# Batch 0's softmax and first weight block, the last quarter's products in halves, and one output transfer on GpSimd's queue

## The chip, the cores and the metric

The kernel runs on one core of one Trainium2 chip. The metric is the device time of one execution in microseconds (us). Three executions of the kernel before took 265.26, 265.31 and 265.31 us, median 265.31 us. The trace and the profile page are of one further execution, which took 265.6 us; the span in its records, from the first instruction to the last, is 263.6 us. All times inside the kernel are us from the start of that span.

## The reference

Linear attention is followed by a two-layer perceptron. There are 8 batches, 8 heads, 576 rows and head dimension 64, so that the model dimension is 512; the hidden dimension is 2048.

```python
def _attn_ref(q, k, v):
    q_s = np.exp(q - max_over_d); q_s = q_s / (sum_over_d + 1e-09)
    k_s = np.exp(k - max_over_s); k_s = k_s / (sum_over_s + 1e-09)
    kv = np.einsum('bhsd,bhse->bhde', k_s, v)
    return np.einsum('bhsd,bhde->bhse', q_s, kv)

def _moe_ref(x, g_ln, w_ch1, w_ch2):      # x: (8, 576, 512)
    mu, var = mean and variance of x over its last axis
    xn = (x - mu) / np.sqrt(var + 1e-06) * g_ln
    ch = np.maximum(xn @ w_ch1, 0.0) @ w_ch2
    return x + ch
```

All inputs and the output are float32.

## The kernel before

**Tiling.** Each batch has 512 main rows, kept as 128 partitions by T = 4 quarters; the remaining 64 rows of all eight batches are collected in a ninth batch, C9, which is worked on last. The products run in bf16. The program walks over the batches 0 to 7 and C9; `run` (L775) merges a list of main steps (the matmuls of the MLP, each with a weight that stands for its duration) with a list of side jobs (attention of the next batch, loads, weight preparation), each with the place at which it is put between the main steps. The order on every engine is that of the program text as it is recorded (L1026).

**Queues.** SyncE (SP) issues q's first half and the four quarters of k of batch 0 (L901, L912), later loads, DMA transposes and half of the last stores. ScalarE (ACT) issues g and the other half of the last stores. GpSimd (POOL) issues, in this order: v of batch 0 in three pieces (L931), q's second half (L901), w1 in five pieces that are cast to bf16 on the way (two of 256 columns, three of 512, L92), w2 and the loads of batch 1 and 2, and later the output of batches 0 to 7 (L474, L561). Each of these queues keeps its order.

**The front (first_batch, L888 to L989).** Memsets, then `warm` (L789): matmuls on a scratch tile that keep TensorE running. Then for quarters 0 and 1 `exp_qt` (ACT), the exponentials of k by pairs of heads `exp_k0` (L262), `norm_q` (DVE), transposes of eq on TensorE with a copy to `eqT` by ACT or DVE (`eq_pT`, L877 with `pe_T`, L857), the column sums of k's exponentials (`z0_mm`, L268), g's columns (`g_columns`, L883), the products of keys and values (`kv0_mm`, L284; after every second pair two DVE rows write `kv_sb`, L297), the attention products of quarters 0 and 1 in column halves (`po_half`, L391; ACT copies them to `x`, L402), the centring `xn_out` (L372), and the first transposes to `xnT` (L983).

**The first MLP stage (mlp_steps, L745; mm1_part, L443).** Batch 0's first products go by parts (m0, mn, t0, tn): blocks m0 to m0 + mn of the hidden dimension, quarters t0 to t0 + tn, each over the four 128-row slices ko of w1. The first four parts take blocks 0 to 3 and quarters 0 and 1, two blocks and one quarter at a time. Quarters 2 and 3 pass as side jobs between them (L1045 to L1049): transposes of eq and xn, the sums `z_q` and products `po_mm` (`q0_rest`, L991), and `x_fast` (L380).

**The tail (last_products, L574).** C9's second MLP product runs as seven products of half size (Strassen's form) into PSUM banks a to e. The last product, n = 4, is added to bank a for the third quarter and to a bank d of its own for the fourth, 8 matmuls of 256 columns each; a DVE row (`stt`, L584) adds it to `yl`, and `store` (L589) writes 64 partitions through SP and 64 through ACT.

At the very end every engine drains and meets at a barrier (L1119); SP first checks the semaphores of all transfers one after the other.

Of the kernel before, what the change touches and what calls it, by code (L numbers as in the profile page):

```python
# [20 lines left out]
def kernel(  # L21
# [21 lines left out]
    P = 128  # L43
# [302 lines left out]
    def po_mm(c, t, i):  # L346


        if i == 0:
            pool, tag = (mm_ps, "m") if c == 0 and t >= 2 else (att_ps, "a")  # L350
            pobox["p"] = pobox[c, t] = pool.tile([P, DM], FP32, tag=tag, name="po")
        if c < B:
            nc.tensor.matmul(  # L353
                pobox["p"][:, i * P : i * P + P], eqTs[c][:, t, i, :], kv_sb[:, c, i, :],
                start=True, stop=True,
            )
        else:
            for half in range(2):
                ps = slice(64 * half, 64 * half + 64)
                nc.tensor.matmul(  # L360
                    pobox["p"][ps, i * P : i * P + P], eqTs[c][:, t, i, ps],
                    kv_sb[:, 2 * t + half, i, :], start=True, stop=True,
                )
# [26 lines left out]

    def po_half(t, half):  # L391

        pool, tag = (mm_ps, "m") if half else (att_ps, "a")
        po = pool.tile([P, DM], FP32, tag=tag, name="po")
        for i in range(2):
            j = 2 * half + i
            nc.tensor.matmul(
                po[:, i * P : i * P + P], eqTs[0][:, t, j, :], kv_sb[:, 0, j, :],
                start=True, stop=True,
            )  # L400
        x, st, _, _ = xs[0]
        nc.scalar.activation(  # L402
            x[:, t, DH2 * half : DH2 * half + DH2], po[:, 0:DH2], AF.Copy,
            accum_out=st[:, t, half : half + 1],
        )
# [121 lines left out]
        )[i]  # L527
        nc.vector.tensor_tensor(out=dst, in0=x, in1=y, op=op)  # L528

    def prod(n, bank, t, k, first=False, own=False):  # L530

        at = slice(t * P, t * P + P)
        if n in (1, 2, 4):
            odd, half = ((0, 0), (1, 0), None, (1, 1))[n - 1]
            lhsT = hbox["h"][:, 2 * k + odd, 2 * half + t, :]
        else:
            lhsT = hbox["s"][:, {5: 0, 6: 1, 7: 2, 3: 3}[n], k, at]
        if n in (1, 2):
            rhs = w2_sb[:, 2 * k + n - 1, 0:DH2]
        elif n == 3:  # L540
            rhs = w2_sb[:, 2 * k + 1, DH2:DM]
        else:
            rhs = w2_q[:, {5: 0, 6: 1, 7: 2, 4: 3}[n], k]
        nc.tensor.matmul(hbox[bank][:, t], lhsT, rhs, start=first and (own or t == 0) and k == 0,  # L544
                         stop=k == KH - 1, skip_group_check=True)

    def bank(name):
# [26 lines left out]
    def last_products(product):  # L574
# [4 lines left out]
        def part(t, col):  # L579
            return yl[:, t, DH2 * col : DH2 * col + DH2]  # L580

        def stt(t, col, src, add=None):
            cols = slice(DH2 * col, DH2 * col + DH2)
            nc.vector.scalar_tensor_tensor(  # L584
                part(t, col), in0=src, scalar=rstds[c][:, t : t + 1],
                in1=xs[c][0][:, t, cols] if add is None else add, op0=ALU.mult, op1=ALU.add,
            )

        def store(t0, tn, col):  # L589
            cols = slice(DH2 * col, DH2 * col + DH2)  # L590
            for half, eng in enumerate((nc.sync, nc.scalar)):
                ps = slice(64 * half, 64 * half + 64)
                to = out[2 * t0 + half : 2 * (t0 + tn) - 1 + half : 2, SM:S, cols]
                eng.dma_start(to.transpose([1, 0, 2]), yl[ps, t0 : t0 + tn, cols])
# [8 lines left out]
        def seed_e():  # L603
# [10 lines left out]
        product(7, "a", at={1: [seed_e, lambda: both("b", 2, 1)], 15: [  # L614
            lambda: both("a", 2, 1, True), lambda: stt(3, 0, hbox["a"][:, 1]),
            lambda: store(2, 2, 1)]})
        product(3, "e", at={15: [lambda: both("e", 0, 1), lambda: store(0, 2, 1), own_bank]})
        product(4, "a", ts=(0,), at={7: [lambda: stt(2, 0, hbox["a"][:, 0]), lambda: store(2, 1, 0)]})
        product(4, "d", ts=(1,), own=True, at={
            15: [lambda: stt(3, 0, hbox["d"][:, 1], part(3, 0)), lambda: store(3, 1, 0)]})  # L620

    def mm2_fast(c):

        steps = []

        def product(n, name, first=False, at=None, ts=range(2), own=False, cut=None):
            at = at or {}
            order = [(t, k) for t in ts for k in range(KH)]
            if cut:
                order = [(t, k) for ks in (range(cut), range(cut, KH)) for t in ts for k in ks]  # L630
            for i, (t, k) in enumerate(order):

                def go(t=t, k=k, i=i):
                    if i == 0 and first:
                        bank(name)
                    prod(n, name, t, k, first or own, own)
                    for fn in at.get(i + KH * ts[0], []):
                        fn()

                steps.append((0.5, go))  # L640

        def seed_c():
            bank("c")
# [101 lines left out]
    def mlp_steps(c):  # L745
# [3 lines left out]
        first, parts = [], ()  # L749
        if c == 0:  # L750
            full = range(0)
            parts = ((0, 2, 0, 1), (0, 2, 1, 1), (2, 2, 0, 1), (2, 2, 1, 1), (4, 4, 0, 2), (0, 4, 2, 1),
                     (0, 4, 3, 1), (4, 4, 2, 2), (8, 4, 0, 2), (8, 4, 2, 2), (12, 4, 0, 2), (12, 4, 2, 2))
        else:
            full, parts = range(8, KO2), ((0, 8, 0, 2), (0, 8, 2, 2))
        for m0, mn, t0, tn in parts:
            first += [
                (0.25 * tn, lambda m=m, t0=t0, tn=tn, ko=ko: mm1_part(c, m, t0, tn, ko))
                for m in range(m0, m0 + mn) for ko in range(KO1)
            ]  # L760
# [127 lines left out]
    def first_batch():  # L888
# [43 lines left out]
                v0[:, j : j + jn].rearrange("p j t d -> p j (t d)"), src0(v, j, jn)  # L932
            )
        load_q0(1, nc.gpsimd)
        load_w1(0, 256)
        load_w1(256, 256)
        for nb in range(1, 4):
            load_w1(512 * nb)
        load_w2(0)
# [1 line left out]

        new_eq(0)
        start_x(0)
        warm(31)
        for t in range(2):
            exp_qt(0, t)
        exp_k0(0)
        exp_k0(1)
        norm_q(0, 0)
        norm_q(0, 1)  # L950
        eq_pT(0, 0, nc.scalar)
        g_columns()
        exp_k0(2)
        warm(5)
        z0_mm(0)
        z0_mm(1)
        exp_k0(3)
        eq_pT(0, 1, nc.vector)
        z0_mm(2)
        warm(3)  # L960
        z0_mm(3)
        recip_z()
        for j in range(NP):
            kv0_mm(j)
        warm(2)
        po_half(0, 0)
        warm(3)
        po_half(0, 1)
        po_half(1, 0)
        po_half(1, 1)  # L970
# [55 lines left out]
    with tc.manual_schedule(  # L1026
# [10 lines left out]
        def po_x(c, t):  # L1037
            for i in range(NP):
# [4 lines left out]
            mlp_steps(0),  # L1043
            [
                (2, lambda: (eq_pT(0, 2, nc.scalar), xn_pT(0, 1, nc.vector), eq_pT(0, 3, nc.scalar))),  # L1045
                (2, lambda: (q0_rest(2), x_fast(0, 2))),
                (6, lambda: q0_rest(3)),
                (8, lambda: (xn_pT(0, 2, nc.vector), x_fast(0, 3))),
                (16, lambda: xn_pT(0, 3, nc.vector)),  # L1049
                (22, lambda: square_sum(0, 0)),  # L1050
                (26, lambda: square_sum(0, 1)),
# [13 lines left out]
            + [(103 + 0.4 * j, lambda j=j: cast_v(1, j)) for j in range(2)]  # L1065
            + [(104.5, lambda: prep_kvrem(1))]
            + [(106, lambda: (kv_all(1), start_x(1)))]
            + [(111, lambda: po_x(1, 0)), (113, lambda: po_x(1, 1))]
            + [(116, lambda: po_x(1, 2)), (118, lambda: xn_pT(1, 0, nc.scalar)), (119, lambda: square_sum(1, 0))]
            + [(119.5, lambda: po_x(1, 3)), (123, lambda: xn_pT(1, 1, nc.scalar)), (124, lambda: square_sum(1, 1))]  # L1070
            + [(128, lambda: xn_pT(1, 2, nc.scalar))]
# [52 lines left out]
```

## Time and profile before

| what | value |
|---|---|
| median of three executions | 265.31 us |
| profiled execution | 265.6 us |
| its span | 263.6 us |
| TensorE (PE) busy | 257.4 us, 98% |
| PE weight loads (PEld) | 218.1 us, 83% |
| VectorE (DVE) | 217.4 us, 82% |
| ScalarE (ACT) | 178.8 us, 68% |
| GpSimd (POOL) | 76.0 us, 29% |
| DMA, chain that ended last | 4% |
| granted PE clock | 1.00, 0.89 behind 259.5 us |

How to read it: a profile line of the chain or of the timeline begins with the start and the duration in us, then the engine, the source line (L451 is line 451 of the kernel before), the operation with output and input, and the number of instructions merged into it; in brackets stands the idle time before it and what ended it. In the table of stages a line holds the stretch, its length, the busy time of PE, PEld, DVE, ACT and POOL with the number of instructions, the granted clock, the busy share of the DMA engines and GB/s. A DMA issue line gives the number of issues, KB of each, and the median us from issue to landing. PE rows overlap: a 128-column matmul is shown with some 0.22 us, though the next one starts 0.055 us later.

### The profile page before, as it was taken

How to read it: one execution, taken by the hardware profiler on the slowest of the kernel's cores; microseconds unless marked ns; L12 is line 12 of the kernel's file. 1: busy time of each engine (PE TensorE's matmuls, PEld its weight loads, DVE VectorE, ACT ScalarE, POOL GpSimd, SP SyncE). 2: the span in 40 equal slices, each digit the busy share in tenths (PEclk: the TensorE clock that was granted, in tenths of full speed). 3: DMA queues.
4: the chain of work that ended last, by engine and by line, in shares of the span. 5: the costliest groups of instructions: out<-in, count | busy, mean ns of one | idle time of the engine just before them, and what ended most of it. 6: DMA issues, size and time to landing. Idle time of an engine off the chain costs nothing.

```text
span 263.6 us, 6818 instructions
## 1 busy us (share of the span) xinstructions
PE 257.4 (98%) x2708; PEld 218.1 (83%) x2711; DVE 217.4 (82%) x475; ACT 178.8 (68%) x350; POOL 76.0 (29%) x126
## 2 busy tenths in 40 slices
PE   8989999999999999999999999999999999999993
PEld 5778855775988998899889988998899888888882
DVE  4667797968989997989798979997999889877873
ACT  4467852896966888688868886788678377438400
POOL 8652316203049007600760076008200300030000
PEclk9999999999999999999999999999999999999999
DMA  6999999997986995799879957997804620521014
GB/s 219 256 204 208 338 208 315 271 155 233 207 151 197 325 136 97 197 308 155 93 215 298 139 99 237 297 135 146 256 6 79 161 82 12 71 90 72 0 42 119
DMA packets 69847, 45.00 MB, mean 171 GB/s; under 512 B 41460, under 2 KB 66040, under 8 KB 69816
## 3 DMA queue, kind: packets, MB, share of 16 engines
q1 hardware_dynamic: 48896, 21.76, 39.3%
q0 software_dynamic: 20320, 22.29, 38.9%
q10 hardware_dynamic: 600, 0.53, 0.6%
q8 instruction: 21, 0.34, 0.6%
q14 instruction: 10, 0.08, 0.1%
HBM read 36.70 MB, written 9.44 MB: 175 GB/s over the span
## 4 chain that ended last, share of the span: by engine, by line
PE 92%; DMA 4%; POOL 2%; issue 0%; ACT 0%; DVE 0%; POOLq 0%
PE ba L544 21%; PE bx L688 19%; PE bb L688 9%; PE ph L451 8%; PE bb L544 5%; PE be L544 5%; PE bc L544 5%; PE pc L497 5%; PE bc L688 5%; DMA w_raw<-in_moe_w_ch_dram 4%; PE ph L436 3%; PE po L353 3%; PE pkv L316 2%; PE ptr L860 1%; POOL v L931 1%; PE po L360 1%
## 5 line engine op out<-in xcount | busy, mean ns | idle before, releaser
L544 PEld LDWEIGHTS <-hs 128*128 128x128 bf16 x512 | 49.5, 98 | 5.7
L688 PEld LDWEIGHTS <-w_q 128*128 128x128 bf16 x448 | 43.1, 98 | 5.2 <-issue 0.2
L544 PEld LDWEIGHTS <-hT 128*128 128x128 bf16 x384 | 37.2, 98 | 4.4
L240 POOL TENSOR_TENSOR tq<-xnT 128x256 bf16<-128x256 bf16 x20 | 12.9, 661 | 78.6 <-DMA xnT<-xn 47.2
L688 PEld LDWEIGHTS <-w1g 128*128 128x128 bf16 x336 | 32.2, 98 | 3.9
L544 PE MATMUL ba<-w_q,hs 128*128 128x256 bf16 x256 | 31.7, 273 | 0.0
L688 PE MATMUL bx<-tq,w_q 128*128 128x256 bf16 x224 | 29.0, 273 | 0.0
L561 POOL DMA_DIRECT2D out_dram<-ot x28 | 15.3, 557 | 46.4 <-DVE ot L555 46.4
L367 ACT ACTIVATE scrap<-x,mv 128x512 bf16<-128x512 bf16 x36 | 25.9, 719 | 1.7 <-DVE x L383 1.3
L383 DVE SCALAR_TENSOR_TENSOR x<-po,rq 128x512 bf16<-128x512 f32 x34 | 23.3, 685 | 1.2 <-PE po L353 1.1
L712 ACT COPY bc<-bx 128x512 f32<-128x512 f32 x28 | 15.2, 594 | 13.0 <-PE bx L688 13.0
L719 DVE TENSOR_TENSOR bb<-bx,s 128x512 f32<-128x512 f32 x28 | 18.2, 694 | 6.3 <-ACT s L716 6.3
L730 ACT ACTIVATE hT<-bc 128x512 bf16<-128x512 f32 x28 | 15.3, 595 | 11.9 <-PE bc L688 11.9
L202 DVE TENSOR_REDUCE zq<-eq 128x16 f32<-128x1024 bf16 (+1 forms) x20 | 20.6, 1049 | 2.3 <-ACT eq L193 2.3
L528 DVE TENSOR_TENSOR hs<-hT 128x1024 bf16<-128x1024 bf16 x32 | 20.9, 674 | 0.9 <-ACT hT L730 0.5
L730 ACT ACTIVATE hT<-bb 128x512 bf16<-128x512 f32 x28 | 15.2, 595 | 8.8 <-PE bb L688 8.8
L353 PE MATMUL po<-kv_sb,eqT 128*128 128x128 bf16 x120 | 20.5, 219 | 0.0
L722 DVE TENSOR_TENSOR hT<-bx,s 128x512 bf16<-128x512 f32 x28 | 18.0, 684 | 3.0 <-PE bx L688 3.0
L569 ACT COPY s<-ba 128x512 f32<-128x512 f32 x15 | 8.7, 579 | 12.5 <-PE ba L544 7.8
L544 PE MATMUL ba<-w_sb,hT 128*128 128x256 bf16 x128 | 16.7, 273 | 0.0
L544 PE MATMUL bb<-w_q,hs 128*128 128x256 bf16 x128 | 16.6, 273 | 0.0
L497 PE MATMUL pc<-w_sb,hT 128*128 128x512 bf16 x61 | 15.6, 379 | 0.2
(135 smaller groups left out, 536.9 us busy)
## 6 DMA issues: line engine op xcount, KB each, us to landing
out_dram<-ot POOLq DMA_DIRECT2D x32, 256.0 KB, 5.9
qt<-in_q_dram SPq DMA_DIRECT2D x5, 1024.0 KB, 7.1
kt<-in_k_dram SPq DMA_DIRECT2D x5, 1024.0 KB, 15.0
vt<-in_v_dram POOLq DMA_DIRECT2D x7, 512.0 KB, 14.3
w_sb<-in_moe_w_ch_dram POOLq DMA_DIRECT2D x4, 512.0 KB, 16.1
qt<-in_q_dram POOLq DMA_DIRECT2D x2, 1024.0 KB, 14.8
kt<-in_k_dram POOLq DMA_DIRECT2D x2, 1024.0 KB, 14.3
w_raw<-in_moe_w_ch_dram POOLq DMA_DIRECT2D x3, 512.0 KB, 13.1
```

The costliest lines, as they stand in the source:

```text
L202: nc.vector.reduce_sum(eqs[c][1][:, ts], eqs[c][0][:, ts], axis=AX.X)
L353: nc.tensor.matmul(pobox["p"][:, i * P : i * P + P], eqTs[c][:, t, i, :], kv_sb[:, c, i, :], start=True, stop=True,)
L367: nc.scalar.activation(scrap, x[:, t], AF.Square, bias=mv[:, t, 0:1], scale=-float(DM), accum_out=mv[:, t, 1:2],)
L383: nc.vector.scalar_tensor_tensor(x[:, t].rearrange("p (h d) -> p h d", h=H), in0=pobox[c, t].rearrange("p (h d) -> p h d", h=H), scalar=1. ...
L451: nc.tensor.matmul(ph[:, m % 2, at : at + tn], (w1g if c else w1_sb)[:, ko, m * P : (m + 1) * P], xnTs[c][:, t0 : t0 + tn, ko, :], start=( ...
L497: nc.tensor.matmul(hbox["pc", t], hbox["h"][:, ko, t, :], w2_sb[:, ko, :], start=(ko == 0), stop=(ko == KO2 - 1),)
L528: nc.vector.tensor_tensor(out=dst, in0=x, in1=y, op=op)
L544: nc.tensor.matmul(hbox[bank][:, t], lhsT, rhs, start=first and (own or t == 0) and k == 0, stop=k == KH - 1, skip_group_check=True)
L688: nc.tensor.matmul(dst[:, q], lhsT, rhs, start=first and q == 0 and ko == 0, stop=ko == 1, skip_group_check=True)
L719: nc.vector.tensor_tensor(out=at[g, "b"], in0=at[g, "x"], in1=at[g, "s"], op=ALU.add)
L722: nc.vector.tensor_tensor(out=h_out(g, 1, 1), in0=at[g, "x"], in1=at[g, "s"], op=ALU.add)
L730: nc.scalar.activation(h_out(g, odd, half), at[g, name], AF.Relu)
```

## The change

- In the front the warm matmuls are divided anew (16, then g's columns, then 16, and fewer later); all four exponentials of k stand together ahead of the first eqT copy on ACT; both eqT copies are made by ACT; the sums z of all four pairs come ahead of the second transposes of eq; and the products of keys and values go pair by pair with warm matmuls between them. `po_half` of quarter 1 takes its PSUM tiles from the pool mm_ps, `po_mm` of batch 0 from att_ps.
- w1's first 512 columns come in two pieces by rows (ko 0 and 1, then ko 2 and 3), not by columns.
- The first MLP products of quarters 0 and 1 run by halves of ko: all four blocks with ko 0 and 1, then all four with ko 2 and 3. The side jobs between them move from places 2, 2, 6, 8 to 2, 4, 8, 8.
- Batch 1's first attention product moves from place 111 to 111.7.
- The last eight matmuls of 256 columns become sixteen of 128, by column halves, and the DVE row behind them becomes two rows of 128 columns; the first stands behind the first eight.
- The store of quarters 0 and 1, second column half, of C9 is issued by GpSimd for both partition halves, not by SP and ACT.

```diff
     def po_half(t, half):
-        pool, tag = (mm_ps, "m") if half else (att_ps, "a")
+        pool, tag = (mm_ps, "m") if half or t else (att_ps, "a")
...
-    def prod(n, bank, t, k, first=False, own=False):
+    def prod(n, bank, t, k, first=False, own=False, ch=None):
...
+        dst = hbox[bank][:, t]
+        if ch is not None:
+            cols = slice(P * ch, P * ch + P)
+            dst, rhs = dst[:, cols], rhs[:, cols]
...
+        def last_half(half):
+            cols = slice(P * half, P * half + P)
+            nc.vector.scalar_tensor_tensor(
+                yl[:, T - 1, cols], in0=hbox["d"][:, 1, cols], scalar=rstds[c][:, T - 1 : T],
+                in1=yl[:, T - 1, cols], op0=ALU.mult, op1=ALU.add,
+            )
...
-        def store(t0, tn, col):
+        def store(t0, tn, col, engs=(nc.sync, nc.scalar)):
...
-        product(3, "e", at={15: [lambda: both("e", 0, 1), lambda: store(0, 2, 1), own_bank]})
+        product(3, "e", at={15: [lambda: both("e", 0, 1), lambda: store(0, 2, 1, (nc.gpsimd, nc.gpsimd)), own_bank]})
...
-        product(4, "d", ts=(1,), own=True, at={
-            15: [lambda: stt(3, 0, hbox["d"][:, 1], part(3, 0)), lambda: store(3, 1, 0)]})
+        product(4, "d", ts=(1,), own=True, half=0, at={15: [lambda: last_half(0)]})
+        product(4, "d", ts=(1,), own=True, half=1, at={15: [lambda: last_half(1), lambda: store(3, 1, 0)]})
...
-            parts = ((0, 2, 0, 1), (0, 2, 1, 1), (2, 2, 0, 1), (2, 2, 1, 1), (4, 4, 0, 2), (0, 4, 2, 1),
+            parts = ((4, 4, 0, 2), (0, 4, 2, 1),
...
+            first += [
+                (0.25, lambda m=m, t=t, ko=2 * kh + ko: mm1_part(c, m, t, 1, ko))
+                for t in range(2) for kh in range(2) for m in range(4) for ko in range(2)
+            ]
...
-        load_w1(0, 256)
-        load_w1(256, 256)
+        for kh in range(2):
+            ks = slice(2 * kh, 2 * kh + 2)
+            nc.gpsimd.dma_start(w1_sb[:, ks, 0:512], w1_src[:, ks, 0:512])
...
-        warm(31)
+        warm(16)
+        g_columns()
+        warm(16)
         for t in range(2):
             exp_qt(0, t)
-        exp_k0(0)
-        exp_k0(1)
+        for j in range(NP):
+            exp_k0(j)
         norm_q(0, 0)
         norm_q(0, 1)
+        z0_mm(0)
         eq_pT(0, 0, nc.scalar)
...
+        z0_mm(1)
+        warm(3)
+        z0_mm(2)
+        z0_mm(3)
+        eq_pT(0, 1, nc.scalar)
+        recip_z()
+        kv0_mm(0)
+        kv0_mm(1)
+        warm(1)
+        kv0_mm(2)
+        warm(2)
+        kv0_mm(3)
+        po_half(0, 0)
         warm(5)
...
-                (2, lambda: (q0_rest(2), x_fast(0, 2))),
-                (6, lambda: q0_rest(3)),
-                (8, lambda: (xn_pT(0, 2, nc.vector), x_fast(0, 3))),
+                (4, lambda: (q0_rest(2), x_fast(0, 2))),
+                (8, lambda: (q0_rest(3), xn_pT(0, 2, nc.vector), x_fast(0, 3))),
...
-            + [(111, lambda: po_x(1, 0)), (113, lambda: po_x(1, 1))]
+            + [(111.7, lambda: po_x(1, 0)), (113, lambda: po_x(1, 1))]
```

## The prediction

> **What bounds the kernel now.** I read the table of stages first, then the chain that ended last, then the waits of the first 22 us, the DMA answers of short windows, and the last rows of every engine. All times are us from the start of the span of before.
>
> ```profile
> 0.00:15.24 15.24, 13.71 (x219) 10.19 (x220) 8.19 (x25) 7.95 (x18) 11.10 (x23) 1.00 0.99 232
> 15.24:21.04 5.80, 5.53 (x81) 4.85 (x81) 4.33 (x13) 3.07 (x6) 2.55 (x3) 1.00 1.24 207
> 21.04:31.80 10.76, 10.76 (x116) 9.86 (x117) 7.26 (x14) 8.39 (x20) 2.71 (x4) 1.00 1.16 276
> 77.00:247.00 170.00, 169.98 (x1773) 150.99 (x1771) 149.26 (x317) 124.84 (x245) 48.06 (x79) 1.00 0.69 151
> 259.50:264.00 4.50, 0.00 (x0) 0.00 (x0) 0.43 (x1) 0.00 (x0) 0.00 (x0) 0.89 0.42 117
> ```
>
> The second column is the length of a stage, the third TensorE's busy time. From 21 to 259.5 TensorE is busy all the time, so a shorter front or a shorter tail comes out in full. No other place of this kernel can pay.
>
> ```profile
> 5.78 9.41 DMA w_raw<-in_moe_w_ch_dram
> 15.24 0.73 PE ph L451 x8
> 16.24 0.59 ACT eqT L862
> 16.88 0.25 PE zs L872 x4
> 21.04 0.40 PE ptr L860 x4
> 258.54 0.89 PE bd L544 x8
> 259.45 0.48 DVE yl L584
> ```
>
> These are pieces of the chain: TensorE starts the MLP at 15.24 when w1's first piece lands (5.78 + 9.4 = 15.2), stands from 16.64 to 16.88 for ScalarE's copy of eqT, and from 20.86 to 21.04 for `xn`; behind the last product come one VectorE row of 0.48 and 3.7 of stores and checks.
>
> ```profile
> 8.37 1.42 ACT L266 ACTIVATE ek<-kt 128x576 bf16<-128x576 f32 x2
> 10.85 1.30 PE L291 MATMUL pkv<-v,ek 64*64 64x64 bf16 x72
> 20.63 0.35 DVE L375 TENSOR_SCALAR xn<-x,mv 128x512 bf16<-128x512 bf16 x1
> q0 software_dynamic: 378, 0.20, 141.5%
> q0 software_dynamic: 208, 0.21, 125.5%
> L1119 POOLq DRAIN  x3: 51/93/6313, 236.4 to 263.3; - x3
> ```
>
> The first three rows are used below. The q0 lines are GpSimd's DMA queue from 12 to 13 (packets of 512 B) and from 17 to 18 (1024 B). The last is GpSimd's drain at its end: 6.3 us.
>
> **The change, part by part.**
>
> *Softmax of the keys, products by pairs.* k's last quarter is issued at 2.8 and lands 6.3 later, at 9.1; ScalarE's last exponential so ends at 9.8 in both kernels (8.37 + 1.42). Before, the 18 z matmuls behind it start only at 10.54 and the 72 products run from 10.85 to 12.09 (17 ns each). After: z at 9.84 (18 of 18 ns, to 10.17), four transposes (0.23, to 10.4), 36 products to 11.05, one warm matmul (0.11), 18 products to 11.47, two warm matmuls (0.22), the last 18 from 11.69 to 12.00. v's pieces land at 9.9, 10.5 and 11.4 (issued 2.96 to 4.4, 6.7 to 7.0 each), so none is late. VectorE's second pair of kv rows (0.59) starts at 12.16 and not 12.25. The four ScalarE copies of `po` follow it: the second starts at 13.11 and not 13.20. So this part is worth only **0.09** at the first half of xnT: it is ready at 15.0, before at 15.1. The warm matmuls are 52 for 53; ScalarE's two eqT copies now stand behind the exponentials (9.8 to 11.0), and nobody asks for them before 12.0.
>
> *w1's first block in row halves.* Per piece 256 descriptors of 1024 B written, before 512 of 512 B. From the q0 lines 512 small packets take 512/378 = 1.35, 256 large ones 256/208 = 1.23: 0.12 a piece. Packet time alone (1.415 x 16 / 378 = 60 ns against 1.255 x 16 / 208 = 97 ns) would give 512 x 60 / 16 = 1.9 against 1.55, 0.35 a piece; nothing gained is the other end. I take 0.12, since the queue's rate is what a landing follows. First piece at 15.1, second (15.9 before) at 15.7. TensorE starts at 15.14: **0.10** gained. The eight matmuls of the first half need only the first half of xnT, so the wait of 0.13 inside the first eight (15.81 - 15.24 - 8 x 0.055) goes.
>
> *Order of the next 5 us.* After the first eight matmuls (0.44, to 15.6) come the three groups of transposes; the middle one waits for `xn` of quarter 1 (15.8, VectorE) to 15.85, the third ends at 16.3. The eight matmuls of the second half (to 16.73) now stand where TensorE waited for eqT (ready 16.5). zs and po: 0.33, to 17.06; sixteen matmuls of 55 ns to 17.94; zs and po to 18.27; xnT's third transposes wait for `xn` (17.28 + 0.70 + 0.39 = 18.37) and end at 18.62, where before stood 19.10. The next sixteen (1.76) need w1's second block, landed at 18.4 before and 18.2 now. VectorE's row for xnT, `x` and `xn` (0.69 + 0.70 + 0.37) follows the transposes, so `xn` of quarter 3 ends at 20.55, before at 20.98. **Gain of the front 0.45**; between 0.1 (only the first step) and 0.65 (that step and the three waits whole, 0.13 + 0.24 + 0.18).
>
> What is late next: the w1, w2 and q loads come only 0.2 earlier. Batch 1's krem lands at 41.35 and its exponential ends at 41.9; TensorE would want it at 42.05 (42.49 before). That is the smallest cover, and it holds.
>
> *po_x at 111.7.* One more mm2 stands ahead of batch 1's first po, which waited 0.14 for kv (43.84 to 43.98). I take **0.1**, between 0 and 0.14. The pools of po and po_half change; the built order shows no wait on a late reader for them.
>
> *The tail.* Column halves: sixteen matmuls of 55 ns for eight of 109, the same 0.87. VectorE's row of 256 columns is 0.48, of 512 columns 0.69, so 128 columns by that slope 0.375 (0.24 if it halved, 0.48 if it did not shrink). The first half lies beside the second's matmuls; the last row ends at 259.83, not 259.93: **0.1**. ScalarE issued its last store at 260.25 because two others were queued; with one store moved away both queues issue at 259.86. Each takes 2.2 to 2.3 to land, so 262.2 or a little later, before 262.26 and 262.45. SyncE then runs down a list of checks: before, the last store was second of nine lines, and the eight from there took 262.26 to 262.76. After, the last stores are seventh and eighth, so the list ends 0.2 to 0.3 sooner for the same landing. Together **0.3** (0 to 0.45).
>
> *A store on GpSimd.* Both halves (128 KB each) of one store are issued at 258.61 and 259.15, 0.54 each. Quiet GpSimd stores of 256 KB landed 2.6 to 4.2 after issue (four rows at 234 to 237); with 2.8 the second is down at 262.0, ahead of the last stores. Cost nothing, if GpSimd's drain then ends soon.
>
> *Sum.* 0.45 + 0.1 + 0.3 = 0.85. The profiled execution took 265.6 (span 263.6), so 264.75; against the median of 265.31, 264.46. I forecast **264.5**, own range 264.1 to 264.9.
>
> **The rivals.**
>
> *GpSimd's drain sets the end (slower).* The last barrier needs all engines' drains. The 6.3 of the row run from 236.4 to 242.7, while the last GpSimd store landed at 240.6 and was issued by 236.94. In before this is over 20 us ahead of the end. Now it stands behind stores issued to 259.7. If it ends 2.1 behind the last landing: 262.0 + 2.1 + 0.8 (SyncE's drain to the span's end) = 264.9 for 263.6, less 0.55 of the front and po: **266.0**. If it is 5.7 behind the issue: 265.4 + 0.8 = 266.2, less 0.55: **267.4**. It decides as soon as the drain ends over 0.5 behind the landing. For it: the row itself. Against: one row, on an engine whose spans the page calls rough; nothing waited for its end; and that transfer itself took 4.2 where the three before it took 2.6 to 2.9, so what the 2.1 is, is not shown. The other two drains of GpSimd are 0.05 and 0.09. I give 0.22 and 0.12. The Trainium skill (VectorE: DVE Perf Modes, "The DRAIN you can't avoid") says that the runtime's boilerplate drains on all five engines are a constant of about 12 ns; by that rule this rival would vanish and the sum would stay at 264.5; the row of 6313 ns speaks against the rule.
>
> *The front's gain is not passed on* (w1's second block, with 0.35 of cover, or krem, with 0.15, is late; or the halves land as before and VectorE's `xn` holds the pace): 264.9 with the tail, 265.3 without. 0.12.
>
> *The change does not do what it says*: pairs as v lands gain little, since k's last quarter sets z. I have counted it so already.
>
> **How the numbers follow.** Forecast 0.50, drain behind the landing 0.22, behind the issue 0.12, front lost 0.12, rest 0.04. The range 264.0 to 266.6 holds the forecast, the lost front and the first drain case. 0.2%, 0.53 us, is about what a measurement of this kernel can tell from no change. Faster (under 264.78): 0.41, most of the forecast. Same (to 265.84): 0.24, the forecast's weak end, the lost front, part of the first drain case. Slower: 0.35, the drains.
>
> **What would show it.** Right: the first ph at 15.1, no idle TensorE from 16.3 to 16.9, the 128x256 matmuls at 18.6, xnT's fourth transposes at 20.6, the last VectorE row of 0.38, GpSimd's last drain over before SyncE's. Wrong: GpSimd's drain as the last to arrive; first ph later than 15.2; TensorE waiting for w1 at 18.6; z later than 10.2.

## The result and the profile after

The change made the kernel slower: 267.32 us, median of six executions (267.05 to 268.82), against 265.31 us of the kernel before beside it (265.26 to 265.65). The ratio is 1.0085, 95% interval 1.006 to 1.011. The profiled execution took 267.18 us, its span is 265.3 us.

In this trace the front came out nearly as forecast (why, is another matter; see below). The stage from 15.24 to 21.04, in the table of stages of the kernel after (columns as above: length, busy time of PE, PEld, DVE, ACT, POOL, granted clock, DMA share, GB/s):

```profile
15.24:21.04 5.80, 5.73 (x86) 5.01 (x85) 4.30 (x13) 3.27 (x7) 2.19 (x3) 1.00 1.24 207
258.00:266.00 8.00, 1.19 (x18) 0.89 (x15) 1.32 (x4) 0.00 (x0) 1.26 (x2) 0.71 0.36 93
```

TensorE is busy 5.73 us of this stage, before 5.53. The first ph (`ph` is the PSUM tile of the first MLP product) starts at 15.14 (before 15.24), its 128x256 matmuls, those of two quarters at once, at 18.80 (19.10), and the DVE row that closes the third quarter stands at 258.17 (258.58). So the changed kernel reached the tail 0.40 sooner; this is called its lead. In the second line, 1.26 us of POOL are new: the issues of two transfers. The tail in the timeline of the kernel after (start, duration, engine, line, operation):

```profile
257.97 0.61 PE L547 MATMUL bd<-w_q,hT 128*128 128x128 bf16 x8
258.17 0.48 DVE L594 SCALAR_TENSOR_TENSOR yl<-ba,rstd,x 128x256 f32<-128x256 f32 x1
258.47 1.26 POOL L604 DMA_DIRECT2D out_dram<-yl  x2 [21.93 <-DVE yl L594]
258.62 0.35 DVE L587 SCALAR_TENSOR_TENSOR yl<-bd,rstd,yl 128x128 f32<-128x128 f32 x1
...
259.02 0.61 PE L547 MATMUL bd<-w_q,hT 128*128 128x128 bf16 x8 [0.44 <-DVE yl L587]
...
259.67 0.35 DVE L587 SCALAR_TENSOR_TENSOR yl<-bd,rstd,yl 128x128 f32<-128x128 f32 x1 [0.70 <-PE bd L547]
```

Two things went against the forecast. First, the second column half does not follow the first: TensorE stands for 0.44 until VectorE has read the first half, and the last row ends at 260.02, later than before (259.93) in spite of the lead. Second, GpSimd's issues end at 259.74, and behind them comes its drain. The instructions of the program's last line in the kernel after (shortest, median and longest duration in ns, first and last start):

```profile
L1135 SPq EVENT_SEMAPHORE  x11: 17/28/1362, 260.6 to 265.3; - x11
L1135 POOLq DRAIN  x3: 51/102/5297, 258.9 to 264.7; - x3
L1135 SPq DRAIN  x3: 7/7/13, 262.8 to 264.5; - x3
```

GpSimd's first drain starts at 258.908 and takes 5297 ns: it ends at 264.205. SyncE's list of checks (its longest, 1362 ns, waits for GpSimd's second transfer) is over at 262.8, and the last barrier then waits 1.4 for GpSimd. After that barrier SyncE's last semaphore comes 0.42 behind GpSimd's, before 0.10.

### The profile page after: what moved, and what is told of

Its sections match the earlier page's. It is cut to its first block, busy times and chain, and to the rows that moved or that the text cites. A ratio compares the mean times of both kernels' runs of the same rounds, so it can differ in the third digit from the quotient of the medians.

```text
span 265.3 us, 6833 instructions
## 1 busy us (share of the span) xinstructions
PE 257.1 (97%) x2715; PEld 218.0 (82%) x2718; DVE 217.0 (82%) x475; ACT 179.5 (68%) x351; POOL 77.1 (29%) x128
```

## The experiments

Each kernel ran beside the kernel before on one chip; "ratio" is against that, with its 95% interval. The experiments ran in five sets, and the median of the kernel before was 265.52 to 265.59 in each. The clock of an execution is TensorE's mean granted clock. Line numbers are those of each kernel and differ by a few.

**1. The store back on SyncE and ScalarE.** The change, with:

```diff
-            store(0, 2, 1, (nc.gpsimd, nc.gpsimd))
+            store(0, 2, 1)
```

> The change, with the one store of the tail put back from GpSimd's queue to SyncE's and ScalarE's; the column halves stay. Theory (GpSimd's drain, 2.1 behind the landing of its last store, sets the end): GpSimd's last drain starts near 236 again and is over by 243; the last VectorE row ends at 260.0 as in the changed kernel, 0.1 later than before, so the time is 265.1 to 265.5. Rival (the column halves are the cause, the drain only fills the time): 266.8 to 267.4. Rival (three stores on two queues at the end are what the GpSimd queue saved): later than before by 0.3 or more, 265.6 to 266.0.

Measured: 267.06 (266.62 to 267.56), ratio 1.0062 (1.005 to 1.0074). The drain did go back (237.6 to 244.0), yet the time did not follow. The trace shows why; stages of this kernel:

```profile
7.35:10.76 3.41, 2.86 (x101) 2.24 (x99) 1.95 (x5) 2.37 (x5) 2.31 (x4) 1.00 1.19 251
10.76:14.17 3.41, 3.41 (x69) 2.40 (x62) 1.16 (x4) 0.71 (x3) 2.23 (x3) 0.50 1.17 228
14.17:17.00 2.83, 2.17 (x24) 1.64 (x23) 1.45 (x5) 2.30 (x9) 1.65 (x2) 1.00 1.24 206
```

The last column but two is the granted clock: for 3.41 us, in the middle of the front, it is 0.50. First ph comes at 16.93, 1.8 late. So the time falls into the range of the rival that blames the column halves, but by another cause, and this run says nothing yet on the drain; it is run again below (12).

**2. Whole columns, store on GpSimd.** The change without the column halves:

```diff
-        product(4, "d", ts=(1,), own=True, half=0, at={15: [lambda: last_half(0)]})
-        product(4, "d", ts=(1,), own=True, half=1, at={15: [lambda: last_half(1), lambda: store(3, 1, 0)]})
+        product(4, "d", ts=(1,), own=True, at={
+            15: [lambda: stt(3, 0, hbox["d"][:, 1], part(3, 0)), lambda: store(3, 1, 0)]})
```

> The change, with the last quarter's product and its VectorE row whole again; the store stays on GpSimd's queue. Theory (GpSimd's drain sets the end): GpSimd's issues, landing and drain stand where they stood, 267.0 to 267.4, although the last VectorE row ends at 259.5 and not at 260.0. Rival (column halves are the cause): 264.9 to 265.3. Rival (both share it, since the late last stores hold up GpSimd's): 266.0 to 266.8.

Measured: 267.46 (267.2 to 268.84), ratio 1.0088 (1.0069 to 1.0106). The last row ends at 259.92, 0.4 later than expected (the front of this execution had no lead), the drain at 264.62. The time is the theory's within 0.1: the column halves are not the cause.

**3. The front alone.** Both edits of the tail undone, as in 1 and 2.

> The change without both edits of the tail: the front, and batch 1's first po at 111.7. Theory (the lead of 0.40 that the last quarter had in the changed kernel is passed on): last VectorE row ends at 259.53 for 259.93 before, and the time is 264.8 to 265.0. Rival (the lead is a matter of one execution, or is lost behind the last row): 265.2 to 265.4.

Measured: 265.63 (265.31 to 266.92), ratio 1.0011 (0.9999 to 1.0022). Against the theory, and over the rival's 265.4 too: the front as a whole gains nothing. In this trace k's last exponential ends at 9.96 (9.35 in the changed kernel), and first ph comes at 15.75.

**4. Column halves in two banks.** The front, halves as in the change, but

```diff
+            hbox["f"] = att_ps.tile([P, 2, DH2], FP32, tag="a", name="bf")
...
-        product(4, "d", ts=(1,), own=True, half=1, at={15: [lambda: last_half(1), lambda: store(3, 1, 0)]})
+        product(4, "f", ts=(1,), own=True, half=1, at={15: [lambda: last_half(1), lambda: store(3, 1, 0)]})
```

> The front, and the column halves with the second half in a PSUM tile (and bank) of its own; all stores on SyncE's and ScalarE's queues. Theory (in the changed kernel the second half waits 0.44 for VectorE's read of the first, because both are in one bank): no such wait, the second half's matmuls follow at once; eight of 128 columns took 0.61 there, so the last row of 0.35 ends between 259.4 (if 0.17 of the 0.61 is only their start) and 259.6; 264.7 to 265.0. Rival (it is the loading of the weights that holds the second half up): the idle time in front of the second half stays, the last row ends at 260.0, 265.2 to 265.5.

Measured: 265.44 (264.98 to 266.91), ratio 1.0004 (0.9991 to 1.0016). Its timeline:

```profile
258.51 0.61 PE L547 MATMUL bd<-w_q,hT 128*128 128x128 bf16 x8
...
258.74 2.19 ACTq L604 DMA_DIRECT2D out_dram<-yl  x3
258.95 0.61 PE L547 MATMUL bf<-w_q,hT 128*128 128x128 bf16 x8
...
259.60 0.35 DVE L587 SCALAR_TENSOR_TENSOR yl<-bf,rstd,yl 128x128 f32<-128x128 f32 x1
```

The wait is gone: the second eight start 0.44 behind the first (8 x 0.055), and from the third quarter's row to the end of the last row it takes 1.24, with whole columns 1.36, with both halves in one bank 1.85. So sharing the tile, and with it the bank, made the wait. The time is nevertheless the rival's, 265.2 to 265.5, and not the theory's: the end did not move against experiment 3 (both spans 263.7), since ScalarE's last issue starts at 260.38, 0.43 behind the row; its three issues fill 2.19 us from 258.74.

**5. GpSimd's store alone.** The kernel before, with the store of experiment 1 on GpSimd's queue and nothing else.

> The kernel before, with one edit only: the store of output columns 256 to 511 of rows of quarters 0 and 1 on GpSimd's queue. Theory (GpSimd's drain ends 2.1 behind the landing of its last store, and the last barrier waits for it): as in the run with whole columns, GpSimd's drain runs to 264.2 to 264.8 and the time is 267.0 to 267.6, 1.6 to 2.1 over before. Rival (the drain costs that much only with the new front around it): under 266.0. Rival (drain at a fixed 5.7 behind the last issue): it would end near 265.8, and the time 268 or more.

Measured: 267.70 (267.54 to 268.15), ratio 1.0077 (1.0061 to 1.0093): 2.16 over the kernel before, as much as the whole change lost. The last line's instructions in this kernel:

```profile
L1119 POOLq DRAIN  x3: 51/93/5458, 259.1 to 265.1; - x3
L1119 SPq DRAIN  x3: 7/7/13, 263.1 to 264.9; - x3
```

GpSimd's drain ends at 264.60 (259.146 + 5.458), 1.48 behind SyncE's at 263.13. The span is 2.09 longer than before: 1.48 for the drain; 0.30 in the last barrier step (0.40 for 0.10); and some 0.5 more between the last row and SyncE's drain (3.36 for 2.84: the last two stores land 2.95 and 3.11 behind their issue, before 2.29 and 2.21), less 0.16 by which this execution's last row came sooner.

**6. Column halves alone.** The kernel before with the halves of the change.

> The kernel before, with the column halves of the last quarter alone, both in one PSUM bank, all stores on SyncE and ScalarE. Theory (bank shared, so the second half waits for VectorE's read; last VectorE row 0.49 later; of this the tail gives 0.33 back, since the last stores no longer queue behind two others): 265.4 to 265.8. Rival (the 1.4 that this kernel's changed form lost against the front alone came from the halves and not from the lower clock of 10.9 to 14.3): 266.6 to 267.1.

Measured: 265.61 (265.45 to 265.87), ratio 0.9999 (0.999 to 1.0008). The wait of TensorE at the end of this kernel (waited for, us, times, longest):

```profile
PE bd L548 <- DVE yl L588: 0.4, 1, 0.4
```

The last row comes 0.49 later against the third quarter's, and from it to the end of the span 3.32 pass, before 3.66. The halves cost nothing that can be told from the noise: by then ScalarE's queue is free, and its last issue starts 0.03 behind the row, before 0.31.

**7. The new order of the keys alone.** The kernel before, with the order of first_batch from `warm(16)` to `po_half(0, 0)` and the PSUM pool of po_half.

> The kernel before, with the new order of the keys' softmax, the products by pairs and the warm-up matmuls alone (first ph still behind w1's first piece, as before). Theory (this order leaves TensorE idle while k lands, 0.4 to 1.1 in 6 to 10, and in some executions the granted clock then falls to half for over 3): median 265.2 to 265.7 but a wider spread than before's 265.3 to 266.0, some runs 266.3 to 267 at a mean clock under 0.995; the profile shows idle TensorE between 6 and 10. Rival (the clock has nothing to do with this order): spread as before, all at 0.997 or more.

Measured: 265.53 (265.41 to 267.32), ratio 1.0013 (0.9996 to 1.0029). Three of twelve executions are at 266.85 to 267.32 with clocks of 0.992 and 0.993, the other nine at 265.41 to 265.94.

**8. w1's halves alone.** The kernel before with the other part of the front: w1 in row halves, the new order of the first products and side jobs, batch 1's po at 111.7.

> The kernel before, with w1's first block in row halves, the new order of the first products (and of the next 5 us), and batch 1's first po at 111.7; keys and warm-up as before. Theory (this is the part of the front that pays: TensorE's 128x256 matmuls come 0.3 sooner, the warm-up stays dense): 264.9 to 265.2, spread as narrow as before's. Rival (k's landing, and krem's in 31.8 to 49, set the pace in both, so the lead is lost): 265.2 to 265.6 with a TensorE idle time of 0.2 to 0.4 in 31.8 to 49.

Measured: 265.20 (265.01 to 266.46), ratio 0.9986 (0.9974 to 0.9997). This part pays.

**9. A denser warm-up.** Experiment 3 with

```diff
+        warm(4)
         z0_mm(0)
...
         z0_mm(2)
+        warm(4)
         z0_mm(3)
```

> The front alone (as in the run with the front only), with eight more warm-up matmuls in TensorE's idle time: four ahead of the first z, four between the third and the fourth. Theory (the new key order leaves TensorE too idle for one interval of 3.41 us in some executions, and the clock then falls to half for the next 3.41, worth 1.2 to 1.5): at most one run of twelve over 266.3, median 264.9 to 265.4 (eight matmuls of 0.11 fit in the 0.3 to 1.1 of idle time, so the pace changes by under 0.2). Rival (the outliers come from k's landing or from elsewhere): three of twelve over 266.3 as there, median 265.6.

Measured: 266.25 (265.26 to 266.64), ratio 1.0017 (1.0006 to 1.0028). No clock under 0.996, as the theory of the clock has it, but the pace is lost: from the end of k's last exponential to the first ph 6.05 pass, 5.79 without the eight. The forecast that they fit in was wrong. These 0.26 are less than the 0.6 by which the median is above experiment 3's; the rest is open.

**10. An earlier store on GpSimd.** The kernel before, with

```diff
-            lambda: store(2, 2, 1)]})
+            lambda: store(2, 2, 1, (nc.gpsimd, nc.gpsimd))]})
```

> The kernel before, with another store of the tail on GpSimd's queue: that of output columns 256 to 511 of quarters 2 and 3, whose data are ready at 256.8, 1.75 sooner. Theory (drain ends 2.1 behind the landing of GpSimd's last store; landing 3.0 behind the second issue): second issue at 257.5, landing near 260.5, drain over at 262.6, before SyncE's list of checks at 262.75: 265.3 to 265.7, no change. Rival (fixed 5.7 from the end of the last issue, 258.1): drain over at 263.8, and 266.3 to 266.8. Rival (a GpSimd store anywhere in the tail costs the same): 267.5 to 267.9.

Measured: 265.58 (265.32 to 266.93), ratio 1.0004 (0.9993 to 1.0015).

```profile
L1119 POOLq DRAIN  x3: 51/93/5142, 257.5 to 263.2; - x3
```

It ends at 262.65 (257.506 + 5.142), and SyncE's at 262.62: the drain just misses the path. The last barrier step takes 0.40 here too, so that step is not tied to a late drain. All five points together:

| kernel | last GpSimd issue over | last landing | drain over | behind landing | behind issue |
|---|---|---|---|---|---|
| before | 236.94 | 240.58 | 242.67 | 2.09 | 5.73 |
| after | 259.74 | 262.12 | 264.21 | 2.08 | 4.47 |
| 2, whole columns | 260.12 | 262.53 | 264.62 | 2.09 | 4.50 |
| 5, store alone | 259.97 | 262.43 | 264.60 | 2.17 | 4.63 |
| 10, earlier store | 258.33 | 260.31 | 262.65 | 2.34 | 4.32 |

The drain follows the landing by 2.1 to 2.3, while its distance from the issue varies by 1.4.

**11. A better tail.** Experiment 8 with the halves of experiment 4 and the middle store as one transfer of 128 partitions:

```diff
-            lambda: store(2, 1, 0)
+            lambda: store_one(2, 0, nc.sync)
...
+            eng.dma_start(out[2 * t : 2 * t + 2, SM:S, cols], yl[:, t, cols])
```

> The front of the run with w1's halves alone (keys and warm-up as before), column halves with the second half in its own bank, and the middle store of the tail as one transfer of 128 partitions on SyncE instead of two halves on both queues, so that ScalarE has one issue less in front of its last. Theory (in before ScalarE's last store is issued 0.28 behind the last VectorE row because two others are ahead of it, and so a shorter last row alone gained nothing): last row ends 0.11 sooner than with w1's halves alone (259.4), both last issues within 0.05 of it, SyncE's list over 0.3 to 0.4 sooner: 264.75 to 264.95. Rival (the last landing is set by the transfers, not by the issue): 265.1 to 265.3, as with w1's halves alone.

Measured: 268.11 (267.77 to 268.4), ratio 1.0097 (1.0084 to 1.011). The last row does end at 259.23. But DMA issues of the last 8 us (KB each, median us from issue to landing) and the DMA busy share, in tenths, from 257 to 265 in 40 slices:

```profile
DMA  0018999920059889920160557853111111000000
...
out_dram<-yl ACTq DMA_DIRECT2D x1, 64.0 KB, 5.1
out_dram<-yl SPq DMA_DIRECT2D x1, 64.0 KB, 5.4
```

From 262.6 to 263.8 a tenth of the 16 engines is still at work, and the last stores land 5.1 and 5.4 behind their issue, where they took 2.2 and 2.3 in experiment 8. The joined transfer has an outer dimension of only two. That it was therefore spread over few engines, with the last stores behind it, is argued, not shown.

**12. Experiment 1 again.** The same kernel.

> The first experiment's kernel once more (the change with the store put back from GpSimd's queue, column halves kept), since it came out 1.4 above the front alone while the halves alone cost 0.07. Theory (its excess was the clock at half for 3.4 us, which falls by chance on about one execution in three): median 265.5 to 265.9, up to five of twelve runs over 266.4. Rival (this kernel itself makes the dip frequent, or the halves cost more with this front): median over 266.4 again.

Measured: 266.46 (265.4 to 267.96), ratio 1.0037 (1.0017 to 1.0058). Six of twelve have clocks of 0.989 to 0.993 and take 266.99 to 267.96; the other six have 0.996 and more and take 265.4 to 265.92. So the clock is the excess, here and in four of experiment 1's five executions; the fifth, 266.62 at a clock of 1.0, is not explained. The rival's number (a median over 266.4) came true, not the theory's. The two sets of this kernel have the low clock in 10 of 17 executions, the other kernels with the new order of the keys in 11 of 48; why this one, with experiment 3's front, has it more often is open.

**13. Halves and a joined last store.** Experiment 8 with the halves of experiment 4; no store for the third quarter's first columns, `store(2, 2, 0)` behind the last row instead.

> The front with w1's halves alone (keys and warm-up as before), column halves with the second in its own bank, and the tail's last two stores of each queue (columns 0 to 255 of quarter 2 and of quarter 3) joined into one per queue, issued behind the last row. Theory (the last issue on ScalarE waits 0.28 for the issue ahead of it, and no transfer is long): last row ends 0.11 sooner than with w1's halves alone, both last issues stand within 0.05 of it, 0.39 sooner, and the transfer of 128 KB lands 2.5 to 2.9 after its issue where 64 KB took 2.4 to 2.5: 264.8 to 265.1. Rival (the larger transfer gives it all back): 265.2 to 265.4.

**14. The joined store, whole columns.** Experiment 8 with only that.

> The front with w1's halves alone, the last quarter's columns whole, and the two last stores of each queue joined into one. Theory: the last issues stand within 0.05 of the last row's end, ScalarE's 0.28 sooner than with w1's halves alone; 264.9 to 265.15. Rival (the larger transfer gives it all back): 265.2 to 265.4.

Measured: 265.38 (265.13 to 266.43), ratio 0.9994 (0.9981 to 1.0007), and 265.49 (265.29 to 266.11), ratio 0.9995 (0.9985 to 1.0005). Both issues stand 0.03 behind the row, yet from the row's end to the span's 3.91 pass in both, 3.67 in experiment 8: the larger transfer, which lands 2.5 to 2.8 behind its issue, gives it back, as the rival had it.

**15. Later kv products.** Experiment 3 with batch 1's kv products at 107 for 106 and its first po at 112.7. Before it, the waits of TensorE between 30 and 65 had shown in experiment 7:

```profile
PE pkv L316 <- ACT ekr L171: 0.3, 1, 0.3
```

> The front only (the third experiment's kernel), with batch 1's kv products and the first po behind them one step of the schedule (0.2) later. Theory (these products waited 0.2 to 0.31 for the loads of v and k in four traces with this front, and lost what the front had gained): no such wait in the trace; the runs at full clock come at 265.1 to 265.5 where they were 265.3 to 265.8; the others, two or three in ten, 1.3 to 1.5 above. Rival (the wait only moves to the po behind, or the loads matter elsewhere): 265.3 to 265.8 at full clock.

Measured: 266.38 (265.36 to 267.42), ratio 1.0025 (1.0008 to 1.0041); five of twelve at 0.991 to 0.994. The wait is gone in this trace, as forecast, but there is no gain: the five fastest, 265.36 to 265.52, are no better than experiment 3's, and two more at full clock take 266.28 and 266.47.

**16. A sparser warm-up.** The kernel before without two lines:

```diff
-        warm(5)
         z0_mm(0)
...
-        warm(3)
         z0_mm(3)
```

> The kernel before without eight of its 53 warm-up matmuls: the five ahead of the first z and the three between the third and the fourth; nothing else is changed, and no product is left out. Theory (a sparse TensorE between 6 and 10 is what lets the clock fall): two to six of twelve runs 1.0 to 1.7 above the rest, at a mean clock under 0.995, the rest at 265.2 to 265.6. Rival (it is the order of the keys, not the density): all within 265.2 to 266.0, as before.

Measured: 265.97 (265.59 to 267.35), ratio 1.0017 (1.0003 to 1.003). Ten of eleven at 0.987 to 0.993, more often than expected, but at a smaller price: the median of the ten is 0.4 over the kernel before, where 1.0 to 1.7 was expected. Its stages:

```profile
8.00:9.00 1.00, 0.81 (x40) 0.72 (x36) 0.76 (x2) 1.00 (x3) 0.81 (x2) 1.00 1.22 207
9.00:10.00 1.00, 1.00 (x54) 0.90 (x53) 0.49 (x2) 0.40 (x1) 0.65 (x1) 0.94 1.23 216
10.00:11.00 1.00, 1.00 (x46) 1.00 (x42) 0.26 (x2) 0.00 (x0) 0.95 (x3) 0.50 1.10 377
```

The clock falls to 0.50 at 9.89 and is back at 13.30, again 3.41 later. In the 3.41 us ahead of the fall TensorE is busy for 3.22, with seven warm matmuls, eight transposes, 72 matmuls of 64x1 for z and ten kv products of 64x64. In experiment 13's trace the 3.41 us from 4.08, where the clock has just risen, are busy for only 2.00, with warm matmuls alone, and the clock holds. So the rows' busy share is not what the clock goes by; taking eight large warm matmuls away was enough, with the order of the keys as before.

**17 and 18. w1's halves again, and with later kv products.** Experiment 8's kernel once more, and with the edit of experiment 15.

> The kernel with w1's halves alone, once more. Theory (it pays): 0.2 to 0.45 under the kernel before in the same set of runs, 265.1 to 265.4 if that stands at 265.55. Rival (the gain was the luck of one set): within 0.15 of the kernel before.

> The kernel with w1's halves alone, with batch 1's kv products and the first po behind them one step of the schedule (0.2) later. Theory (in one of three traces with this front these products waited 0.2): 0.05 to 0.15 under w1's halves alone, 265.0 to 265.3. Rival (what is gained there is lost at the po behind it): as w1's halves alone.

Measured: 265.13 (264.95 to 265.39), ratio 0.9981 (0.9968 to 0.9994), and 265.42 (264.99 to 266.94), ratio 1.0001 (0.9982 to 1.0019). The first repeats its gain, 0.39 under the kernel before. The later kv products do not help; in that trace they waited 0.3 again. Why is open.

## Why the prediction was wrong, by its steps

**The step that failed: "Cost nothing, if GpSimd's drain then ends soon".** It did not end soon. Experiment 5 puts 2.16 on this edit alone, which is all of the change's loss (2.0). The rival "GpSimd's drain sets the end", 2.1 behind the last landing, was the right mechanism, and its chance of 0.22 was too small: the row of 6313 ns already stood 2.09 behind the last landing. I held against it that the page calls this engine's spans rough, that nothing waited, and that one transfer was slow. None of these is evidence that a drain would be shorter at the end. The forecast of that rival, 266.0, was 1.3 too low. 0.3 is the last barrier step. 0.7 is the second transfer, which landed at 262.12 and not at 262.0 less 0.55: the lead was 0.40, GpSimd's first issue came 0.3 behind the row that releases it where I had 0.03, its issues took 0.63 and not 0.54, and the second landed 3.0 behind its issue and not 2.8. The other 0.3 is that I set the span of an execution of 265.6 beside the median of 265.31.

The row was weighed against the Trainium skill (VectorE: DVE Perf Modes, "The DRAIN you can't avoid"), by which the drains that the runtime puts around a program are a constant of about 12 ns. The drains here stand under the program's own last line, so the sentence need not mean them. The runs decide for the row: SyncE's drains took 7 to 13 ns, but GpSimd's first took 5142 to 6313 ns in the five traces of the table.

**Column halves, forecast 0.1 sooner: wrong in sign at the row, and no matter at the end.** "The first half lies beside the second's matmuls" fails, since both are in bank d (0.44 of wait; gone in experiment 4). The size of the row was right: 0.35, forecast 0.375. What the step also missed is that the last row is not what the end of the kernel before hangs on. Experiment 4 shortened it and gained nothing; experiment 6 lengthened it by 0.49 and lost nothing that can be told. There ScalarE's last issue is what counts: from its start to the end of the span 3.30 to 3.36 pass in twelve of the thirteen traces whose stores are those of the kernel before (3.46 in experiment 16), wherever the row ends. "Both queues issue at 259.86" was the right part of the 0.3: both issues did follow the row by 0.03. "Each takes 2.2 to 2.3 to land" was not: with GpSimd's store the last ones took 2.3 and 2.5 in the changed kernel and 2.9 to 3.1 in experiments 2 and 5.

**The front, forecast 0.45, gave nothing as a whole; its parts were mis-sized.** *The order of the first products held.* From the first ph to the 128x256 matmuls 3.57 to 3.75 pass in the fourteen traces with the new order, 3.83 to 3.89 in the six with the old one. From the fourth xnT to the third quarter's row experiment 8 takes 0.14 less, which fits po_x at 111.7 (forecast 0.1). With these parts alone the kernel gained 0.34 and 0.39 in two sets of runs.

*The 0.10 for w1's first piece is not seen.* It landed at 13.60 to 15.14 in the fourteen traces with row halves and at 13.41 to 15.32 in the six with column halves. That the first ph stood at 15.14, as forecast, was luck. TensorE's rows of before, then of after:

```profile
15.24 0.73 PE L451 MATMUL ph<-xnT,w_raw 128*128 128x128 bf16 x8 [0.28 <-DMA w_raw<-in_moe_w_ch_dram]
```

```profile
15.14 0.66 PE L450 MATMUL ph<-xnT,w_raw 128*128 128x128 bf16 x8 [0.28 <-DVE xnT L1001]
```

In the changed kernel w1 had landed at 14.30, and the ph waited for VectorE's xnT; that came early because k's last quarter landed at 8.65 and not at 9.08.

*The term that failed is the one of 0.09 for the keys.* TensorE's timeline of before, then of after:

```profile
10.54 0.44 PE L274 MATMUL z<-ones,ek 64*64 64x1 bf16 x18
10.85 1.30 PE L291 MATMUL pkv<-v,ek 64*64 64x64 bf16 x72
```

```profile
9.41 0.44 PE L274 MATMUL z<-ones,ek 64*64 64x1 bf16 x18 [0.39 <-ACT ek L266]
9.78 0.40 PE L875 MATMUL ptr<-ident,eq 128*128 128x128 bf16 x4
10.11 0.76 PE L291 MATMUL pkv<-v,ek 64*64 64x64 bf16 x36
10.80 0.28 PE L808 MATMUL warm<-junk 128*128 128x256 bf16 x1
11.01 0.47 PE L291 MATMUL pkv<-v,ek 64*64 64x64 bf16 x18
11.41 0.39 PE L808 MATMUL warm<-junk 128*128 128x256 bf16 x2
11.74 0.47 PE L291 MATMUL pkv<-v,ek 64*64 64x64 bf16 x18
12.14 0.28 PE L396 MATMUL po<-kv_sb,eqT 128*128 128x128 bf16 x2
```

By starts, the 72 products in one piece take 1.24 (10.85 to 12.09); in three pieces they take 0.69, 0.40 and 0.40, and the one and two warm matmuls between them 0.21 and 0.33 where I had 0.11 and 0.22. From z's start to the last 18 products I had 1.85; it is 2.33, and the excess of 0.48 lies in steps of 0.04 to 0.11 where small products and large matmuls take turns. So the path from k's last exponential to the first ph is 5.79 in all seven traces with the new order at full clock and the same warm-up, and 5.30 to 5.62 in ten at full clock with the old one: some 0.3 lost where 0.09 was to be gained.

The premise that the last exponential ends at 9.8 in both kernels failed too, in the other direction. In the new order it starts 0.02 to 0.03 behind the landing of k's last quarter; in the old one 0.02 to 0.85 behind it, because a copy of eqT, which itself waits 0.51 for TensorE's transposes in the trace of before, stands between the exponentials on ScalarE. Counted from that landing, the first row of xnT ends 6.34 or 6.35 later in the seven traces with the new order, and 5.87 to 6.89 later, 6.3 in the mean, in nine with the old one. So the keys' part as a whole neither gains nor loses, and experiment 7 alone was level with the kernel before (265.53 for 265.54). Why the front as a whole, 265.63 in experiment 3, then does not show the gain of w1's halves is open. A part may be what the prediction called the smallest cover: in six traces, none of them of a kernel with the old front, batch 1's kv products waited 0.17 to 0.32 for their inputs (2, 4, 7, 12, 13 and 18), so a lead of the front did not come out in full.

That the changed kernel's trace had 0.40 of lead is k's landing: its last exponential ended at 9.35, in the trace of before at 9.79, and in the seven traces with the new order this ranges from 8.90 to 9.96. Two single traces were no ground for a tenth.

**The clock was no step at all, and should have been.** A clock of 0.994 or less marks the interval at half (3.41 x 0.5 of some 260 is 0.0066 of the mean). Leaving out the kernels whose end waited for a late transfer, since a longer end lowers the mean too, and experiments 9 and 16:

| kernels | executions at 0.994 or less |
|---|---|
| new order of the keys (1, 3, 4, 7, 12, 15) | 21 of 65 |
| old order (before; 6, 8, 10, 13, 14, 17, 18) | 2 of 220 |
| new order, eight more warm matmuls (9) | 0 of 12 |
| old order, eight fewer (16) | 10 of 11 |

In experiments 7 and 12 such an execution is some 1.5 us slower than the others. I had counted the warm matmuls (52 for 53) and costed their division at nothing. Experiment 7 moves the warm matmuls and the products together, so it does not tell which of the two moves matters; experiments 9 and 16 show that the warm matmuls do. The slower executions of the changed kernel (268.21 and 268.82) fit this, but the one that was traced ran at full clock until 261.36, behind its last product.

The Trainium skill (TensorE: Matmul & The Clock Gate, "What's actually happening") has the clock halved after an idle window of 3413 ns, free-running. The interval agrees (10.76 to 14.17 in experiment 1), and the warm matmuls first ran at 0.11 and not 0.21 apart from a point between 3.9 and 7.1 on, by trace, as a free-running window would have it. "Idle" does not: the interval ahead of the fall was busy for 2.86 of 3.41 in experiment 1 and for 3.22 in experiment 16. What the gate counts, no run here shows.

## What to carry to other kernels

Before an engine with an idle queue gets a last store, look how long its drain takes and behind what it ends: here GpSimd stores whose issue was over 3.6 us before the end of the kernel before cost 2.2, and one whose issue was over 5.3 before it cost nothing that shows in the median. Cost a step on the path by the gaps between kinds of matmul too, and a part of a tail by the queue that issues last, not by the row ahead of it. Warm-up matmuls that seem to fill only idle time can hold the clock: without eight of 53 it fell in ten of eleven executions. And compare medians of many executions, since k's last exponential alone moved between 8.90 and 9.96 from trace to trace.

## What the runs showed of the hardware

- GpSimd's last drain ends 2.1 to 2.3 behind the landing of its last transfer, and the last barrier step took 0.40 to 0.42 for 0.10 in the four traces with a GpSimd store in the tail.
- Two column halves in one PSUM tile, one bank, run one after the other with VectorE's read between them (0.44 of wait); in two tiles they run side by side. The wait is the program's: in the traces of the change and of experiment 6 the first matmul of the second half waits on VectorE's semaphore, and in experiment 4 it waits on none. What the chip would do in one bank without that semaphore, no run here shows.
- In the tail of the kernel before ScalarE's second issue behind a first one took 0.81, SyncE's 0.56, for the same 64 KB; so a third is late there first (0.31 behind the last row, SyncE's 0.03).
- Behind a transfer of 128 KB with an outer dimension of two, a tenth of the 16 engines was at work for 1.2 us, and the stores behind it landed 5.1 and 5.4 behind their issue (experiment 11). Which transfer held them up is argued, not shown.

The fastest version found is that of experiments 8 and 17, the kernel before with w1's halves, their order and the later po: 265.20 and 265.13, faster than both kernels.
